# The down stage of a fused attention and feed-forward kernel: its four blocks take their accumulators in another order

## The chip, the cores and the metric

The kernel runs on one core of a Trainium2 chip. Its metric is the device time of one execution, in microseconds (us), taken as the median of several executions. A hardware profile of one execution gives the times of single instructions. In it PE is TensorE's matmul unit, PEld its weight loads, ACT is ScalarE, DVE is VectorE, POOL is GpSimd and SP is SyncE, which issues most DMAs. The span is the time from the first to the last instruction.

## The reference

Two parts follow each other. The first is a lightning attention with decay over 4 batches, 8 heads, 768 positions and a head width of 64, worked through in blocks with a running state. Its output is laid out as 3072 tokens of 512 numbers. The second is a feed-forward block:

```
out[:, :, sl] = intra + inter           # per block of positions, then kv_state is updated
x = attn_out.transpose(0, 2, 1, 3).reshape(3072, 512)
h = x @ w_in                            # 512 -> 2048
g = np.maximum(0.01 * h, h)
out = g @ w_out                         # 2048 -> 512
```

All is wanted in float32 accuracy; the weights arrive as float64.

## The kernel before

**Three products for one.** A float32 operand is split into a rounded head h, a scaled rest l and a combination m of both. A product of two operands is the matmuls h x h and l x l into one sum, scaled, and m x m into another or the same sum. So a float32 product takes three passes over PE.

**Stages.** The attention runs round by round (4 batches of 6 rounds). The up stage multiplies by `w_in`, applies the leaky ReLU and stores g to DRAM, for 6 groups of 512 tokens and 8 pairs of 128-wide slices of the hidden width (`up(g, p)`, matmul line 628). The down stage loads g back (`down_load`, line 660), splits it (ACT line 669, DVE lines 670 and 672) into a ring of four slots, and multiplies by `w_out` (`down(g, p)`, matmul line 687).

**The down stage.** A call of `down(g, p)` covers the pairs p and p + 1 of group g, for four blocks tb = 0 to 3 of 128 tokens. A block takes 12 matmuls of 512 columns for one call, six for each pair: for each half f of the pair the passes h, l and m. h and l are added into the sum `acc[tb][0]`, m into the sum `acc[tb][1]`, over the four calls of a group. In the last call of a group each block is evicted: ACT scales the first sum into `t` (line 709), DVE adds the second sum to it into `gs` (line 716), and SP stores 128 rows of the output (line 719). Both `t` and `gs` are double-buffered. After the group's fourth call the blocks start over with the next group's rows.

**The very last block** (group 5, last call, tb = 3) is ordered by hand so that its end can be worked on in halves (line 701): first all h and l matmuls of both pairs, eight in all, then the four m matmuls for columns 0 to 255, then those for columns 256 to 511. DVE adds and SP stores its rows in the same two halves.

**Accumulators.** PSUM holds these buffers: `b10`, `b11` and `b2`, one sum of 128 x 512 float32 each, which the up stage uses in rotation; `pt`, of the same size, and `psc` and `po`, each of which has room for two such sums in two halves (`psc[:, 0]` and `psc[:, 1]`). `pt`, `psc` and `po` belong to the attention before. `acc` gives each block its two sums, `ACC` the names under which the planner follows them.

**What sets the order.** Every piece of work is given to a planner (`Plan.add`) with an estimated cost, the names that it reads and writes, and a rank that grows along a list of steps. `Plan.emit` simulates the engines: at each turn it takes the piece that can start earliest, and of those that can start at the same time the one of lowest rank, then of lowest number. The pieces of one `down` call share a rank and are numbered by block. The instructions are then written out in the order of their planned starts. The waits between engines aren't the planner's: the tile framework derives them from the buffers that each instruction, in that written order, reads and writes.

The waits inside the last block come from these lines (the first part is added as usual; the halves read the name of the second sum and write that name with 0 or 1 behind it):

```
699  order = [(one, (0, 1, 2), every), (two, (0, 1, 2), every)]
700  if very_last:
701      order = [(one + two, (0, 1), every)] + [(one + two, (2,), x) for x in halves]
```

Of the kernel before, what the change touches and what calls it, by code (L numbers as in the profile page):

```python
# [36 lines left out]
class Plan:  # L37
# [23 lines left out]
    def add(self, eng, us, fn, reads=(), writes=(), rank=0.0):  # L61

        n, deps = len(self.ops), set()
        for k in reads:
            w, r = self.last.setdefault(k, [None, []])
            if w is not None:
                deps.add(w)
            r.append(n)
        for k in writes:
            w, r = self.last.setdefault(k, [None, []])  # L70
            if w is not None:
                deps.add(w)
            deps.update(r)
            self.last[k] = [n, []]
        deps.discard(n)
        ways = {eng: us} if isinstance(eng, str) else dict(zip(eng, us))
        if self.slack:
            self.more[n] = self.slack
        if self.chain is not None:
            self.chains[self.chain].append(n)  # L80
        self.ops.append((ways, fn, deps, (self.rank + rank, n), set(writes)))
# [81 lines left out]
def kernel(  # L163
# [48 lines left out]
    def ps(shape, name):  # L212
        return psum.tile(shape, F32, name=name, tag=name)


    pt = ps([P, HP, C], "pt")
    psc = ps([P, 2, 2 * HP, C2], "psc")
    po = ps([P, 2, 2 * HP, C2], "po")
    b1, b2 = [ps([P, T], f"b1{i}") for i in range(2)], ps([P, T], "b2")
# [396 lines left out]
    def up(g, p, lo=0, hi=GC):  # L616
# [35 lines left out]
            lambda: nc.sync.dma_start(out=G[g][p].rearrange("p (f t) -> p f t", f=2)[:, :, toks], in_=y), [f"gs{jg}"], [f"G{g}{p}"], slack=GSLACK)  # L652


    acc = [[b1[0], b2], [b1[1], pt.rearrange("p y t -> p (y t)")]] + [
        [z[:, i].rearrange("p y t -> p (y t)") for i in range(2)] for z in (psc, po)]
    ACC = [["b10", "b2"], ["b11", "pt"], ["psc", "psc"], ["po", "po"]]
    ring = [[X[j // 2][z].rearrange("p k t -> p (k t)")[:, j % 2 * 2 * T:(j % 2 + 1) * 2 * T] for z in range(3)] for j in range(NR)]

    def down_load(g, p):  # L660
# [14 lines left out]
    def down(g, p):  # L675

        nonlocal n_t
        for tb in range(GC):
# [3 lines left out]
            def go(pps, zs, cols, tb=tb):  # L682
                for pp in pps:
                    j = (g * NP + pp) % NR
                    for f in range(2):
                        for z in zs:
                            nc.tensor.matmul(acc[tb][z // 2][:, cols], lhsT=ring[j][z][:, f * T + tb * P:f * T + (tb + 1) * P],  # L687
                                             rhs=W[pp][z][:, f * d_model:(f + 1) * d_model][:, cols],
                                             start=pp == 0 and f == 0 and z != 1, stop=pp == NP - 1 and f == 1,
                                             skip_group_check=True)  # L690

            def needs(pps, zs):
                return [f"{x}{z}{y}" for pp in pps for z in zs for x, y in (("r", (g * NP + pp) % NR), ("w", pp))]
# [8 lines left out]
            for pps, zs, cols in order:  # L702
                part_of = f"{halves.index(cols)}" if cols in halves else ""
                add("PE", 0.227 * 2 * len(pps) * len(zs) * (0.53 if part_of else 1.0), lambda pps=pps, zs=zs, cols=cols, go=go: go(pps, zs, cols),
                    needs(pps, ["hlm"[z] for z in zs]) + ([ACC[tb][1]] if part_of else []), sorted({ACC[tb][z // 2] + part_of for z in zs}))
            if done:
                jt, n_t = n_t % 2, n_t + 1
                t, y = tt[jt], gs[jt][:, 0, :]
                add("ACT", 0.6, lambda t=t, tb=tb: nc.scalar.activation(out=t, in_=acc[tb][0], func=AF.Copy, bias=0.0, scale=(1.0 + 1.0 / S) / U),  # L709
                    [ACC[tb][0]], [f"t{jt}"], rank=-1.5)  # L710
                rows = out[(g * GC + tb) * P:(g * GC + tb + 1) * P, :]
                n = 2 if very_last else 1
                for i in range(n):
# [3 lines left out]
                            y[:, cols], acc[tb][1][:, cols], 1.0 / WS, t[:, cols], op0=ALU.mult, op1=ALU.add),  # L717
                        [f"t{jt}", ACC[tb][1]] + ([ACC[tb][1] + str(i)] if n == 2 else []), [f"gs{jt}{i}" if n == 2 else f"gs{jt}"], rank=-1.5)
                    add("DMA", 0.8 / n, lambda rows=rows, y=y, cols=cols: nc.sync.dma_start(out=rows[:, cols], in_=y[:, cols]),
# [83 lines left out]
```

## Time and profile before

| | |
|---|---|
| median of 4 runs | 613.71 us |
| the four runs | 613.15, 613.77, 613.64, 615.08 us |
| profiled execution: its own time | 613.15 us |
| its span | 611.3 us |
| PE busy | 597.3 us (98%) |
| ACT busy | 270.9 us (44%) |
| DVE busy | 313.0 us (51%) |
| matmuls of the down stage | 344.27 us to 607.45 us |
| granted TensorE clock, mean | 0.999 |

A share of busy time is an average over stages. What a change to one place is worth is read from the rows of that place: which instruction ends last there, and what it waited for. The chain that ended last follows the execution back from its last instruction, and gives for each piece the start, the length and the instruction. In a timeline row, the bracket at the end gives the idle time of the engine before the instruction, and the engine whose work ended that wait.

### The profile page before, as it was taken

To read this page: it belongs to the slowest core of one execution; us is meant where nothing else is said; L and a number is where in the kernel's file an instruction comes from. 1 tells how busy PE (TensorE), PEld (TensorE's weight loads), DVE (VectorE), ACT (ScalarE), POOL (GpSimd) and SP (SyncE) were. 2 spreads that over 40 slices of the span, in tenths; PEclk is the share of its full clock that TensorE was granted. 3 is DMA by queue.
4 is the path that set the end of the run, shared out by engine and by line. 5 is a ranking of instruction groups with operands and counts; after the bars stand their busy time and mean duration, and the time that the engine had idled before them with its cause. 6 is when DMAs were issued, how large, how long until landed. Compare 5 with 4: busy or idle time off the path is not lost.

```text
span 611.3 us, 12915 instructions
## 1 busy us (share of the span) xinstructions
PE 597.3 (98%) x5402; PEld 495.4 (81%) x5402; DVE 313.0 (51%) x412; ACT 270.9 (44%) x434; POOL 83.6 (14%) x90
## 2 busy tenths in 40 slices
PE   7799999999999999999999999999999999999997
PEld 5587888888888888888888888888888888888885
DVE  4899980164353444335356745545454545636431
ACT  4688884444465656555576622222312313114111
POOL 1563400134242013113000000000000000000000
PEclk9999999999999999999999999999999999999999
DMA  9999876445789878886775932424333333324101
GB/s 219 221 256 267 240 203 153 139 122 149 177 221 255 221 220 214 231 245 189 281 253 203 316 125 105 170 79 142 125 109 132 114 127 120 130 94 140 68 1 69
DMA packets 141162, 104.66 MB, mean 171 GB/s; under 512 B 117040, under 2 KB 117808, under 8 KB 141104
## 3 DMA queue, kind: packets, MB, share of 16 engines
q1 hardware_dynamic: 136608, 95.44, 52.8%
q10 hardware_dynamic: 4496, 8.39, 4.4%
q8 instruction: 42, 0.69, 0.5%
q14 instruction: 16, 0.13, 0.1%
HBM read 68.16 MB, written 35.65 MB: 170 GB/s over the span
## 4 chain that ended last, share of the span: by engine, by line
PE 92%; DVE 4%; DMA 2%; ACT 0%; SPq 0%; issue 0%; POOL 0%; DVEq 0%; ACTq 0%
PE b L628 42%; PE b L687 18%; PE po L687 11%; PE psc L687 11%; PE po L312 4%; PE pt L687 4%; PE psc L312 3%; DMA att<-in_v_dram 2%; DVE w L572 1%; DVE w L573 1%; PE pt L391 1%; DVE wl L584 0%; DVE wh L581 0%; DVE att L447 0%; PE po L391 0%; DVE wm L590 0%
## 5 line engine op out<-in xcount | busy, mean ns | idle before, releaser
L669 ACT ACTIVATE xh<-att 128x1024 fp32r<-128x1024 f32 x48 | 50.9, 1061 | 146.0 <-PE po L687 144.3
L670 DVE SCALAR_TENSOR_TENSOR xl<-att,xh 128x1024 fp32r<-128x1024 f32 x48 | 58.7, 1223 | 97.9 <-ACT xh L669 97.9
L628 PE MATMUL b<-xl,wl 128*128 128x512 f32 (+1 forms) x392 | 102.8, 386 | 0.6 <-DVE wl L584 0.6
L628 PE MATMUL b<-xh,wh 128*128 128x512 f32 (+1 forms) x392 | 102.7, 386 | 0.8 <-ACT xh L495 0.8
L628 PE MATMUL b<-xm,wm 128*128 128x512 f32 (+1 forms) x392 | 103.2, 391 | 0.0
L628 PEld LDWEIGHTS b<-xh,wh 128*128 128x128 f32 x392 | 72.7, 188 | 16.1 <-ACT xh L495 0.9
L628 PEld LDWEIGHTS b<-xl,wl 128*128 128x128 f32 x392 | 72.5, 188 | 15.7 <-DVE wl L584 1.0
L628 PEld LDWEIGHTS b<-xm,wm 128*128 128x128 f32 x392 | 71.2, 188 | 14.7
L649 ACT ACTIVATE gs<-b 128x512 f32<-128x512 f32 x96 | 57.3, 598 | 47.9 <-PE b L628 43.8
L646 ACT ACTIVATE b<-b 128x512 f32<-128x512 f32 x96 | 56.0, 585 | 50.3 <-PE b L628 50.2
L687 PE MATMUL b<-wh,xh 128*128 128x512 f32 x192 | 74.7, 389 | 0.0
L687 PE MATMUL b<-wl,xl 128*128 128x512 f32 x192 | 74.7, 389 | 0.0
L672 DVE SCALAR_TENSOR_TENSOR xm<-xl,xh 128x1024 fp32r<-128x1024 f32 x48 | 58.8, 1226 | 5.2 <-DVE xl L670 0.5
L440 DVE TENSOR_TENSOR att<-psc,att 128x512 f32<-128x512 f32 x24 | 16.5, 689 | 63.5 <-PE psc L312 63.3
L687 PEld LDWEIGHTS b<-wl,xl 128*128 128x128 f32 x192 | 36.1, 188 | 7.5
L687 PEld LDWEIGHTS b<-wh,xh 128*128 128x128 f32 x192 | 36.0, 188 | 7.5
L407 POOL TENSOR_TENSOR att<-att 128x512 f32<-128x512 f32 (+1 forms) x23 | 26.1, 1136 | 97.6 <-PE po L391 54.3
L572 DVE TENSOR_SCALAR w<-w 128x512 int32<-128x512 int32 x32 | 19.3, 603 | 39.3 <-ACT w L566 39.3
L450 POOL TENSOR_TENSOR att<-att 128x256 f32<-128x256 f32 x40 | 32.3, 808 | 44.1 <-DVE att L447 44.1
L687 PE MATMUL po<-wm,xm 128*128 128x512 f32 (+1 forms) x100 | 37.2, 381 | 0.7 <-ACT raw L709 0.7
L687 PE MATMUL psc<-wh,xh 128*128 128x512 f32 x96 | 37.3, 389 | 0.0
L687 PE MATMUL psc<-wl,xl 128*128 128x512 f32 x96 | 37.3, 389 | 0.0
(73 smaller groups left out, 806.6 us busy)
## 6 DMA issues: line engine op xcount, KB each, us to landing
att<-g SPq DMA_DIRECT2D x48, 512.0 KB, 3.2
g<-gs SPq DMA_DIRECT2D x47, 512.0 KB, 3.8
raw<-in_moe_w_in_dram ACTq DMA_DIRECT2D x16, 512.0 KB, 4.8
raw<-in_moe_w_out_dram SPq DMA_DIRECT2D x16, 512.0 KB, 4.5
att<-in_k_dram SPq DMA_DIRECT2D x48, 128.0 KB, 4.5
att<-in_v_dram SPq DMA_DIRECT2D x24, 256.0 KB, 4.0
out_dram<-gs SPq DMA_DIRECT2D x23, 256.0 KB, 2.0
wo<-w SPq DMA_DIRECT2D x8, 512.0 KB, 5.7
```

The costliest lines, as they stand in the source:

```text
L312: nc.tensor.matmul(dst[HALF[cols]], lhsT=lhsT[HALF[rows]], rhs=rhs[HALF[rows]], start=start, stop=True, skip_group_check=True)
L407: lambda e="POOL": ENG[e].tensor_tensor(kr[nr], kr[nr], _bc(pow_k, 3, D)[nr], op=ALU.mult), ["fk"], [f"k{i}"])
L440: add("DVE", 0.69, lambda: nc.vector.tensor_tensor(sc, psc[:, :, lower, :], decay, op=ALU.mult), ["psc", "fk"], ["sc"])
L450: add("POOL", 0.7, lambda new=new, j=j: nc.gpsimd.tensor_tensor(state[(j + 1) % 4], new, _bc(lam_c, 2, D), op=ALU.mult), [f"st{j % 4}", "f ...
L572: add("DVE", 0.42, lambda: nc.vector.tensor_scalar(d, d, 3, None, op0=ALU.logical_shift_left), [], [key])
L628: nc.tensor.matmul(dst, lhsT=w[z][:, kk * 2 * P + f * P:kk * 2 * P + (f + 1) * P], rhs=x[z][:, kk, toks], start=start and kk == 0, stop=kk ...
L646: add("ACT", ns, lambda b=b: nc.scalar.activation(out=b, in_=b, func=AF.Copy, bias=0.0, scale=S + 1.0), [], [kb], rank=-1.5)
L649: add("ACT", ns, lambda b=b, r=r: nc.scalar.activation(out=r, in_=b, func=AF.Prelu, bias=0.0, scale=1.0 / WS, alpha=0.01), [kb], [f"gs{jg} ...
L669: add("ACT", 1.05, lambda: nc.scalar.activation(out=h, in_=graw[j], func=AF.Copy, bias=0.0, scale=NEAR), reads, wr("h"))
L670: add("DVE", 1.25, lambda: nc.vector.scalar_tensor_tensor(l, graw[j], 1.0, h.bitcast(F32), op0=ALU.mult, op1=ALU.subtract), reads + [f"rh{ ...
L672: add("DVE", 1.25, lambda: nc.vector.scalar_tensor_tensor(m, l.bitcast(F32), -S, h.bitcast(F32), op0=ALU.mult, op1=ALU.add), [f"rh{j}", f" ...
L687: nc.tensor.matmul(acc[tb][z // 2][:, cols], lhsT=ring[j][z][:, f * T + tb * P:f * T + (tb + 1) * P], rhs=W[pp][z][:, f * d_model:(f + 1) ...
```

## The change

The table of accumulators is put in another order. Blocks 0 and 1 now take the halves of `psc` and of `po`, blocks 2 and 3 take `b10` with `b2` and `b11` with `pt`. With it the last block, tb = 3, has its first sum in `b11` and its second in `pt`. Nothing else differs.

```
-    acc = [[b1[0], b2], [b1[1], pt.rearrange("p y t -> p (y t)")]] + [
-        [z[:, i].rearrange("p y t -> p (y t)") for i in range(2)] for z in (psc, po)]
-    ACC = [["b10", "b2"], ["b11", "pt"], ["psc", "psc"], ["po", "po"]]
+    acc = [[z[:, i].rearrange("p y t -> p (y t)") for i in range(2)] for z in (psc, po)] + [
+        [b1[0], b2], [b1[1], pt.rearrange("p y t -> p (y t)")]]
+    ACC = [["psc", "psc"], ["po", "po"], ["b10", "b2"], ["b11", "pt"]]
```

## The prediction

> **What bounds the kernel now.** I read the page's engine table first (PE busy 98% of the span, DVE 51%, ACT 44%), then the waits of PE from 296 us to the end, the busy time by windows, the chain of waits over the last 8 us, and the timeline of the last 11 us. The waits of PE and the down stage's window (columns of the second: the stretch, then busy time and instruction count of PE, PEld, DVE, ACT and POOL, clock, DMA share, GB/s):
>
> ```profile
> PE po L687 <- ACT raw L709: 0.7, 1, 0.7
> 344.00:606.00 262.00, 262.00 (x1158) 216.91 (x1157) 128.40 (x118) 64.13 (x73) 0.00 (x0) 1.00 0.33 115
> ```
>
> From 296 us on PE waits once, for 0.7 us; from 344 to 606 us it is busy for all of the 262.00 us at full granted clock. So in the down stage the matmuls themselves set the time, at one per 0.227 us (603.13, 603.35, 603.58 in the timeline below), and a reordering of the banks can win only where PE stands still. The end of the chain of waits shows that place (start, length, what):
>
> ```profile
> 603.97 2.07 PE po L687 x11
> 606.04 0.02 issue
> 606.06 0.61 ACT raw L709
> 606.67 0.04 issue
> 606.71 0.75 PE po L687 x4
> ```
>
> The last block is cut in three by hand (line 701): eight matmuls of the h and l parts into the first sum, four half-width ones of the m part for columns 0 to 255 of the second sum, and four for columns 256 to 511. PE ends the first half, ACT evicts the first sum, and only then does PE do the second half. PE, ACT and PE stand in a row, and DVE's two half-width additions follow. The timeline of three places says why:
>
> ```profile
> 600.41 0.39 PE L687 MATMUL b<-wl,xl 128*128 128x512 f32 x1
> 600.63 0.39 PE L687 MATMUL pt<-wm,xm 128*128 128x512 f32 x1
> 600.83 0.60 ACT L709 ACTIVATE raw<-b 128x512 f32<-128x512 f32 x1 [2.12 <-PE b L687]
> ...
> 603.13 0.39 PE L687 MATMUL psc<-wl,xl 128*128 128x512 f32 x1
> 603.35 0.39 PE L687 MATMUL psc<-wm,xm 128*128 128x512 f32 x1
> 603.78 0.60 ACT L709 ACTIVATE raw<-psc 128x512 f32<-128x512 f32 x1 [2.35 <-PE psc L687]
> ...
> 605.17 0.39 PE L687 MATMUL po<-wl,xl 128*128 128x512 f32 x1
> 605.39 0.63 PE L687 MATMUL po<-wm,xm 128*128 128x256 f32 x4
> 606.06 0.60 ACT L709 ACTIVATE raw<-po 128x512 f32<-128x512 f32 x1 [1.69 <-PE po L687]
> 606.71 0.74 PE L687 MATMUL po<-wm,xm 128*128 128x256 f32 x4 [0.69 <-ACT raw L709]
> 607.54 0.76 DVE L716 SCALAR_TENSOR_TENSOR gs<-po,raw 128x256 f32<-128x256 f32 x2 [2.44 <-PE po L687]
> ```
>
> Block 1 has its sums in two buffers, b11 and pt. ACT starts at 600.83, which is 0.03 us after the last matmul into the buffer that it reads (600.41 + 0.39 = 600.80), while the m matmul into pt still runs to 601.02. Block 2 has both sums in the buffer psc. ACT starts at 603.78, 0.04 us after the m matmul into the other sum (603.35 + 0.39 = 603.74), and not after its own (603.52). So the program's waits go by buffer. In po this costs twice: ACT's read of the first sum, ready at 605.17 + 0.39 = 605.56, waits for the first m half (606.02), and the second m half, a write to po, waits for ACT's read. The DVE half of columns 0 to 255, whose own matmuls ended at 606.02, waits for the second m half too (607.46).
>
> **The change part by part.** No instruction is added, removed or resized. Blocks 0 and 1 go from b10/b2 and b11/pt to psc and po, blocks 2 and 3 the other way. Rows, weights, order of the blocks, loads and stores stay, so no step passes another on SP's or any other queue by the edit itself; only the planner's choices at the stage's start can move, costed below.
>
> *The tail.* With b11 and pt for block 3, ACT starts at 605.56 + 0.03 = 605.59 and ends at 606.19 (0.60 from its row), beside PE. The second m half has nothing to wait for: pt is not read before. It follows the first half. Within the first half four matmuls take 0.63 from start to end, their starts 0.12 apart (605.39, 605.51, 605.63), so eight take 0.63 + 4 x 0.12 = 1.11, and PE ends at 606.50 instead of 607.46. DVE's first half then starts 0.09 later as now (607.45 to 607.54), at 606.59; ACT's result of 606.19 is there. It still waits for the second m half, because both lie in pt. What leaves the chain is 0.02 + 0.61 + 0.04 of ACT and its issue, and 0.75 - 0.48 = 0.27 of refilling PE: 0.94, by the clock times 607.54 - 606.59 = 0.95. If the second half could not overlap the first and kept its 0.75, PE would end at 606.77 and the gain would be 0.68. If DVE's first half waited only for ACT and the first m half, it would start at 606.19 + 0.07 = 606.26: a gain of 1.28, and its second half, 0.34 later at 606.60, would not be held by PE either. I take 0.95, the row of the first half being the nearest.
>
> *Behind it.* The two DVE halves (607.54, 607.88), two stores issued from 608.00 and the end at 611.3 move as they are. The store of block 2 (in a row of SP's timeline issued at 605.13, landing in about 2.0 us) is over by 607.1; the first moved store is issued near 607.05. The gs buffer that the last block writes was stored for block 1, whose DVE ended at 602.15, so its 2.0 us are over by about 604.5. No new wait there: 0.
>
> *The start of the stage.* Now the planner slips six matmuls of block 2 (psc, 344.27) and six of block 1 (b11, 345.63) between the products of the last up block, then the up block's m product (346.99), and leaves block 0 until b2 is evicted (348.76). After the change psc and po, idle since the attention, serve blocks 0 and 1, so the same gap can be filled at the same time, by block 0 and then block 0 or 1; b10/b2 come later than now, and b2's wait gets longer cover. A gain is excluded, since PE has no idle time there. A loss could come only if the up block's m product were pulled ahead of ACT's scaling, which ends at 345.50, 0.13 before PE's next free place: at most one eviction, 0.6 us. I take 0.
>
> *The group changes.* Five times a block's buffer is written again, 8.16 us (three blocks of 2.72) after its last matmul. The tightest is block 3, whose eviction stands behind conversions of the next group:
>
> ```profile
> 389.41 0.58 ACT L709 ACTIVATE raw<-po 128x512 f32<-128x512 f32 x1
> ...
> 393.12 0.68 DVE L716 SCALAR_TENSOR_TENSOR gs<-po,raw 128x512 f32<-128x512 f32 x1
> ...
> 396.86 0.39 PE L687 MATMUL po<-wh,xh 128*128 128x512 f32 x1
> ```
>
> It ends at 393.80 and PE comes back at 396.86: 3.06 us of cover, 8.16 us of distance for every block in either order. Taken as 0; if the cover went, each microsecond beyond would count five times.
>
> *A rule against the change.* The row: each sum of psc or po is 512 floats wide, in a half of its own, and ACT nevertheless waited 606.06 - 605.59 = 0.47 us for a write to the other half. The Trainium skill, PSUM — Partial Sum Buffer, section "PSUM bank collisions raise a hardware error", asks for semaphores by bank and quadrant, and the page's terms put 512 floats in a bank. By that rule the two sums were in separate banks already, nothing had to wait, and the change would be worth 0; by the rows it is worth 0.95. The same rule asks that DVE's read and PE's write within one bank be kept apart, which would leave the first DVE half waiting for the second m half, as I have it.
>
> *The sum.* The profiled execution took 613.15 with a span of 611.3, so 1.85 lies outside the span. After: span 611.3 - 0.95 = 610.35, execution 612.20. That execution is the fastest of the four, 0.56 under the median of 613.71. On the median: 613.71 - 0.95 = 612.76, or 612.8, which is 0.15%.
>
> **The rivals.**
> 1. *DVE's first half is released early* and the tail gives 1.28: 612.4. For it: its own matmuls end 0.48 earlier. Against: at 607.54 it waited for the second half although its columns were done at 606.02, and pt is one buffer for both.
> 2. *The separation doesn't do what it says:* 613.7. It would need ACT's wait to be something other than the shared buffer. Against are blocks 1 and 2 above, which differ in just that.
> 3. *Slower:* at the five group changes the eviction of block 3 falls behind another pair of conversions on DVE (four at 1.23 us, 4.92), so that b11 and pt come free 4.92 - 3.06 = 1.86 late, five times: 9.3 - 0.95 = 8.4 slower, 622.1. It decides from a delay of 0.44 beyond the cover (5 x 0.44 = 2.2, less 0.95, is 1.25). For it: the planner lays out both queues anew. Against: the block distances and lengths are unchanged, and the next conversion starts only at 397.97 on ACT, when a ring slot comes free.
> 4. *A smaller gain* of 0.3 to 0.7, by the unoverlapped second half or 0.6 lost at the start: 613.0 to 613.4.
>
> **How the numbers follow.** A measurement of this kernel can tell about 0.2%, 1.23 us, from no change. The forecast (a gain of 0.95) has 0.74, rival 1 0.09, rival 2 0.05, rival 3 0.06, rival 4 0.06. The forecast lies only 0.28 inside the bound, and the four runs differ by 0.1 to 0.6 us even without the 615.08; so I give about four in ten of its 0.74 to a time beyond the bound (0.30), the rest to within it (0.44). Of rival 1, 0.07 is beyond and 0.02 within; rivals 2 and 4 are within, less 0.02 for runs as high as 615.08. Faster 0.37, same 0.02 + 0.44 + 0.11 - 0.02 = 0.55, slower 0.08. The range goes from 612.1 (rival 1 less 0.3 of spread) to 613.4 (rival 4's upper end); rivals 2 and 3 and the far ends of the spread are left out.
>
> **What would show it.** Right: in the last block ACT starts about 0.03 after the last l matmul and beside the m halves, PE has no wait after 296 us, eight half-width matmuls follow each other in about 1.1 us, DVE starts 0.09 after the last, and the span is near 610.35. The waits list would lose PE <- ACT. Wrong: an ACT start after the first m half again (rival 2), a DVE start before the last m matmul ends (rival 1), or PE waits for DVE L716 near 396 us and every 43.5 us after (four pairs of 10.88) (rival 3). A change anywhere ahead of 344 us would overturn the reading that the plan is the same up to there.

## The result and the profile after

The changed kernel takes 613.05 us (median of 33 runs, 611.78 to 615.11); the kernel before, in 53 runs, takes 613.9 us. The ratio is 0.9987 with a 95% interval of 0.9982 to 0.9992, which is 0.5 to 1.1 us faster. That is 0.13%, inside the 0.2% that the prediction called no change. The profiled execution took 612.5 us, its span is 610.7 us.

The end of the chain of waits of the changed kernel (start, length, what; DVEq is DVE's sequencer):

```profile
605.89 0.96 PE pt L688 x8
606.86 0.03 DVEq L717
606.89 0.04 issue
606.93 0.42 DVE gs L717
```

ACT is gone from the chain, and the eight m matmuls of the last block are one piece. (All lines of the code are one further down than before.) The timeline of the last block:

```profile
605.50 0.39 PE L688 MATMUL b<-wl,xl 128*128 128x512 f32 x1
...
605.73 1.11 PE L688 MATMUL pt<-wm,xm 128*128 128x256 f32 x8
605.93 0.60 ACT L710 ACTIVATE raw<-b 128x512 f32<-128x512 f32 x1 [1.44 <-PE b L688]
606.93 0.75 DVE L717 SCALAR_TENSOR_TENSOR gs<-pt,raw 128x256 f32<-128x256 f32 x2 [1.73 <-PE pt L688]
```

ACT starts 0.04 us after the last l matmul (605.50 + 0.39 = 605.89) and runs beside the m matmuls. The waits of PE from 296 us on no longer have one on ACT. The one row that is left belongs to the attention:

```profile
PE po L312 <- DVE att L479: 0.3, 1, 0.3
```

It isn't new: the same wait of 0.28 us ends at 295.54 us in the kernel before and, because this execution runs 0.34 us later, at 295.88 us here.

The execution can be cut at three marks that every trace has: the start of the first down matmul, the start of the last l matmul, and the start of DVE's first half. The **stage** lies between the first two, the **tail** between the second and the third, and the **rest** from there to the end of the span. (The page prints the span to 0.1 us; the spans here are the kept traces' own, to 0.01.)

| profiled execution | first down matmul | stage | tail | rest | span |
|---|---|---|---|---|---|
| before | 344.27 | 260.90 | 2.37 | 3.79 | 611.33 |
| changed | 344.61 | 260.89 | 1.43 | 3.79 | 610.72 |

The tail gives 0.94 us. This execution came to the down stage 0.34 us later, through code that the change does not touch, so its span shows only 0.6 of it.

### The profile page after: what moved, and what is told of

It reads as the page before. It is cut to its first block, busy times and chain, and to the rows that moved or that the text cites. A ratio compares the mean times of both kernels' runs of the same rounds, so it can differ in the third digit from the quotient of the medians.

```text
span 610.7 us, 12915 instructions
## 1 busy us (share of the span) xinstructions
PE 597.8 (98%) x5402; PEld 495.5 (81%) x5402; DVE 313.2 (51%) x412; ACT 270.7 (44%) x434; POOL 83.2 (14%) x90
## 4 chain that ended last, share of the span: by engine, by line
PE 92%; DVE 3%; DMA 3%; SPq 0%; issue 0%; POOL 0%; ACT 0%; DVEq 0%; ACTq 0%
PE b L628 42%; PE b L688 18%; PE po L688 11%; PE psc L688 11%; PE po L312 4%; PE pt L688 4%; PE psc L312 3%; DMA att<-in_v_dram 2%; DMA att<-in_k_dram 1%; DVE w L573 1%; DVE wm L590 1%; DVE wl L584 0%; DVE w L572 0%; DVE wh L581 0%; PE po L391 0%; PE pt L391 0%
## 5 line engine op out<-in xcount | busy, mean ns | idle before, releaser
L572 DVE TENSOR_SCALAR w<-w 128x512 int32<-128x512 int32 x32 | 17.1, 533 | 40.2 <-ACT w L566 40.1
L688 PE MATMUL psc<-wm,xm 128*128 128x512 f32 x96 | 37.3, 389 | 0.0
```

What stands on the lines that cost most here:

```text
L572: add("DVE", 0.42, lambda: nc.vector.tensor_scalar(d, d, 3, None, op0=ALU.logical_shift_left), [], [key])
```

## The experiments

Two theories stood against each other from the start. The first: waits go by buffer, and the whole gain is the tail of the last block. The second: the gain comes from elsewhere, from the banks in which the stage begins or from where the sums lie in PSUM. Ratios below are to runs of the kernel before on the same chip; each run's kernel was timed 12 times, the two with the cut in every group 7 and 10 times.

**Another pair of buffers at the end.** (In this run and the next, both tables are built from a list of names; shown is what comes out for one of them.)

```
-    ACC = [["b10", "b2"], ["b11", "pt"], ["psc", "psc"], ["po", "po"]]
+    ACC = [["po", "po"], ["b11", "pt"], ["psc", "psc"], ["b10", "b2"]]      # acc alike
```

> Blocks 0 to 3 take po, b11/pt, psc, b10/b2: the last block has its two sums in two buffers again, but other ones, and the stage begins with other banks than in either kernel. Theory (waits go by buffer, the whole gain is in the tail): from the start of the last l matmul to the start of DVE's first half 1.43 us as in the changed kernel (2.37 before), so 0.94 us faster than before, ratio near 0.9985. Rival (the gain comes from which bank the stage starts in, or from b11 and pt as such): the tail or the stage's length differs from the changed kernel's and the gain is lost or halved, 0 to 0.5 us.

Ratio 0.9979 (0.9967 to 0.9991). The stage took 260.89 and the tail 1.43 us. It is not b11 and pt that matter, and not the banks at the start.

**A new order with the last block in one buffer.**

```
-    ACC = [["b10", "b2"], ["b11", "pt"], ["psc", "psc"], ["po", "po"]]
+    ACC = [["po", "po"], ["b10", "b2"], ["b11", "pt"], ["psc", "psc"]]      # acc alike
```

> Blocks 0 to 3 take po, b10/b2, b11/pt, psc: the order of the buffers is new everywhere, and the last block's two sums share the buffer psc. Theory: the tail of before comes back, 2.37 us from the last l matmul to DVE's first half with PE waiting 0.7 us for ACT, and the time equals that of before within 0.1 us (ratio 1.000). Rival (the gain comes from the stage's new start, or po alone was at fault): 0.5 to 0.95 us faster than before.

Ratio 0.9999 (0.9985 to 1.0012). The end of its chain of waits is that of before, in psc instead of po:

```profile
606.63 0.61 ACT raw L713
607.23 0.04 issue
607.28 0.75 PE psc L691 x4
608.03 0.04 DVEq L720
```

The stage took 260.89, the tail 2.38 us. So all blocks can change their banks and nothing moves as long as the last one keeps its two sums in one buffer. These two runs together show the cause.

**The m matmuls in one go, in the kernel before.**

```
-                order = [(one + two, (0, 1), every)] + [(one + two, (2,), x) for x in halves]
+                order = [(one + two, (0, 1), every), (one + two, (2,), every)]
```

> The kernel before, but the last block's m matmuls are done in one go at full width (four instead of eight; DVE and the stores keep their halves). Theory: PE waits for nothing; ACT's read of the first half of po waits for all four m matmuls, whose last ends 0.22 + 3 x 0.227 + 0.39 = 1.29 us after the last l matmul's start, then ACT 0.60 and DVE: 0.04 + 0.60 + 0.06 later. So 1.99 us from the last l matmul to DVE instead of 2.37: 0.38 us faster than before (ratio 0.9994). If ACT did not wait by buffer, it would run beside the m matmuls and DVE would start after 1.29 + 0.09 = 1.38 us: 0.99 us faster.

Ratio 0.9986 (0.9974 to 0.9997). The interval holds both the 0.9994 of the theory and the 0.9984 of its rival, so the trace decides:

```profile
603.79 2.73 PE po L687 x12
606.52 0.02 issue
606.55 0.60 ACT raw L709
607.15 0.03 issue
607.18 0.42 DVE gs L716
```

ACT waits for all of the m matmuls, as a wait by buffer has it, and the tail is 1.96 us (1.99 expected). So 0.41 of the 0.94 us (2.37 - 1.96) were the price of cutting the m matmuls inside a shared buffer. The other 0.53 (1.96 - 1.43) are ACT standing behind PE instead of beside it, 0.58, less the 0.05 that the cut still costs in the changed kernel (next run).

**The same in the changed kernel.**

> The changed kernel with the last block's m matmuls in one go at full width. Theory (DVE's first half waits for all that is written to pt, so the cut of the m matmuls serves nothing): DVE starts 1.29 + 0.09 = 1.38 us after the last l matmul's start instead of 1.43, 0.05 us faster than the changed kernel, 0.99 faster than before (ratio 0.9984). Rival (the cut lets DVE's first half go early): the first half starts later than 1.43, by up to 0.3 us, and the time is above the changed kernel's by as much.

The edit is the one above. Ratio 0.9983 (0.9972 to 0.9995), tail 1.38 us. The cut of the m matmuls serves nothing in the changed kernel either; without it the tail is 0.05 us shorter. This settles the prediction's first rival: DVE's first half never went early.

**The two sums crossed between blocks 2 and 3.**

```
+    acc_last = acc[:2] + [[acc[2][0], acc[3][1]], [acc[3][0], acc[2][1]]]   # used in group 5
+    ACC_last = ACC[:2] + [["psc", "po"], ["po", "psc"]]
```

> The kernel before, but in the last group blocks 2 and 3 swap their second sums: block 2 has psc[0] and po[1], block 3 has po[0] and psc[1]. Each sum stays in a half of 512 floats of its own, as before; only the buffer that the last block's second sum belongs to is another than its first sum's. Theory (waits go by buffer): ACT's last eviction runs beside the m halves, PE has no wait, DVE's first half starts 1.43 us after the last l matmul instead of 2.37: 0.94 us faster than before (ratio 0.9985). The eviction of block 2 by DVE (its second sum now lies in po) waits until block 3's l matmuls end and starts about 1.2 us later than before, which is not on the path. Rival (the place of the two sums in PSUM counts, not the buffer's name; before, they were in two separate halves already): nothing changes, 0 us.

Ratio 1.0019 (1.0010 to 1.0028): about 1.2 us slower by the ratio, 0.8 by the marks of the trace, which neither theory said. The timeline of PE shows why:

```profile
605.08 0.63 PE L690 MATMUL psc<-wm,xm 128*128 128x256 f32 x4
606.39 0.74 PE L690 MATMUL psc<-wm,xm 128*128 128x256 f32 x4 [0.69 <-ACT raw L712]
607.12 0.51 PE L690 MATMUL po<-wh,xh 128*128 128x512 f32 x1
```

With these names the planner took the h and l matmuls to be held by block 2's eviction and put the two m halves ahead of them. The second half then waited 0.69 us for ACT's read of block 2's sum in the other half of psc, and the eviction of block 3 came last, behind the h and l matmuls. The run tests another written order and not the question, except that the wait of 0.69 us in the shared buffer is there again, for another pair of instructions.

**Crossed, with the order of before.** The buffers are crossed as above, but the planner is told the old names (and, for the group's first call, that block 2 also writes `po`).

> As the crossed kernel (in the last group block 2 has psc[0] and po[1], block 3 has po[0] and psc[1]), but the planner keeps the names of before for them, so that the written order of the last call is that of before: h and l of block 3, then the two m halves. Theory (waits go by buffer): ACT's last eviction starts 0.03 us after the last l matmul's end and runs beside the m halves, PE has no wait, DVE's first half starts 1.43 us after the last l matmul's start instead of 2.37, and the time is 0.94 us below before (ratio 0.9985). DVE's eviction of block 2 reads the half of po next to the one that block 3's h and l matmuls write, so it waits for their end, about 1.2 us later than before. Rival (the place of the sums in PSUM counts): the two sums were in separate halves before and still are, so nothing changes: 2.37 us, 0 us.

Ratio 0.9989 (0.9978 to 1.0000), stage 260.89, tail 1.84 us: a gain of 0.53, neither 0.94 nor 0. PE has no wait and the eight m matmuls follow each other, as the theory has it; the rival is out. The chain shows what was left out of the expectation:

```profile
604.99 2.05 PE po L688 x9
607.05 0.04 DVEq L717
607.08 0.04 issue
607.13 0.70 DVE gs L717
607.83 0.02 issue
607.85 0.61 ACT raw L710
608.46 0.02 issue
608.48 0.42 DVE gs L717
```

DVE's eviction of block 2, whose second sum now lies in po, waited for block 3's h and l matmuls in the other half, as expected. But ACT's eviction of block 3 waited for that DVE instruction too, 0.03 us behind its end, though both only read po. They have one more buffer in common: ACT writes one half of `raw`, which holds both `t`, while DVE reads the other. But in SBUF, the memory that holds `t` and the ring, two halves of one buffer aren't kept apart here. In the same trace ACT writes one ring slot of `xh` while PE reads the slot that is the other half of that buffer:

```profile
388.56 1.06 ACT L669 ACTIVATE xh<-att 128x1024 fp32r<-128x1024 f32 x1 [0.31 <-PE po L688]
388.82 0.39 PE L688 MATMUL po<-wh,xh 128*128 128x512 f32 x1
```

So it is `po` that ACT waits for: the program keeps even two reads apart when they come from two engines and lie in one PSUM buffer. The runs have this in one place only. The Trainium skill, PSUM — Partial Sum Buffer, section "PSUM bank collisions raise a hardware error", lists reads against reads among what must not meet, but within one bank and quadrant; the runs show the waits across the two halves of a buffer, 512 floats each.

**The cut in every group.**

```
-            very_last = done and g == NG - 1 and tb == GC - 1
+            very_last = done and tb == GC - 1        # and the names of the gs halves, so that the order holds
```

> The kernel before, with the last block's order (h and l of both pairs first, then m in two halves, DVE and stores in halves) in block 3 of every group, not of the last alone. It multiplies the disputed wait by about six. Theory (waits go by buffer): at five group changes the second m half waits for ACT's read of po, which stands behind a conversion of 1.06 us that itself waits for block 3's l matmuls; so it starts about 1.06 + 0.60 + 0.1 = 1.75 us after the l matmuls' end instead of 0.48, some 1.3 us lost each time: 5 x 1.3 + 5 x 0.05 for the narrower matmuls = 6.7 us slower than before (range 3 to 12), PE waiting for ACT about six times. Rival (no wait by buffer): 0.3 us slower, no waits.

> The changed kernel with the same order in block 3 of every group. Theory: the first sum is in b11, the second in pt, so PE has no wait at any group change; 0.05 us a group for the narrower matmuls: 0.3 us slower than the changed kernel, about 0.65 us faster than before, and some 7 us faster than the same edit on the kernel before. Rival (the wait is not by buffer): as slow as the same edit on the kernel before.

On the kernel before the ratio is 1.0018 (1.0000 to 1.0037), on the changed kernel 0.9986 (0.9973 to 0.9999). The stage took 261.26 us in both, 0.36 more than without, which is 0.07 for each of the five cuts (0.05 expected). The tails are 2.37 and 1.43. So this expectation failed: the 6.7 us are not there. In the trace of the first, PE waits for ACT only in the last block, in that of the second not at all, and the two differ behind the start of the stage by the 0.94 us of their tails, as the two kernels without this edit do. A group change in the kernel before, with this edit:

```profile
389.30 1.12 PE L687 MATMUL po<-wm,xm 128*128 128x256 f32 x8
...
390.45 0.60 ACT L709 ACTIVATE raw<-po 128x512 f32<-128x512 f32 x1
```

The eight m matmuls run through. At a group change ACT's eviction stands behind two conversions in the plan, so its read is written out after both halves and PE need not wait for it. By the rows ACT starts 0.03 us behind the second half (389.30 + 1.12 = 390.42). In the last block nothing stands before ACT, its read is planned between the halves, and the second half has to wait. The shared buffer alone does not cost PE time; a read written between two writes does.

**Two queues for the last stores.** The changed kernel, m matmuls in one go, and the second output half stored from ACT's queue:

```
+   q = nc.scalar if i else nc.sync      # i: output half; q.dma_start(out=rows[:, cols], in_=y[:, cols])
```

> The changed kernel with the last block's m matmuls in one go, and its second output half stored from ACT's queue instead of SP's. Theory: the tail up to DVE is 1.38 us. SP's second issue stands 0.13 us behind the end of DVE's second half because the first issue takes 0.33 us and more (608.29 to 608.42 before); ACT's queue is free, so the second issue comes about 0.09 us sooner: the part from DVE's start to the end goes from 3.8 to 3.7 us, in all 1.05 to 1.1 us below before (ratio 0.9983). Rival (an issue from ACT costs more, or the two stores then collide): that part stays at 3.8 us or grows, 0.8 to 0.99 below before.

Ratio 0.9975 (0.9962 to 0.9988), median 612.87 us beside 614.45 of before. The second issue now stands directly behind DVE's second half (609.49 + 0.41 = 609.90):

```profile
609.49 0.41 DVE L717 SCALAR_TENSOR_TENSOR gs<-pt,raw 128x256 f32<-128x256 f32 x1
609.61 0.33 SPq L720 DMA_DIRECT2D out_dram<-gs  x1
609.94 0.37 ACTq L720 DMA_DIRECT2D out_dram<-gs  x1
```

Tail 1.39 and rest 3.70 make 5.09 us, beside 5.22 of the changed kernel and 6.16 of before. That is 1.07 us less than before, where 1.05 to 1.1 was expected, and 0.13 less than the changed kernel. The measured times can't tell the last: the intervals overlap.

## Why the prediction was right, and where its terms were off

- *What bounds the kernel.* PE ran through the stage in 260.90 us before and 260.89 after. A reordering could win only in the one wait of PE, and did.
- *The tail.* Predicted: ACT 0.03 us after the last l matmul, eight m matmuls in 1.11 us, DVE 0.09 behind them, a gain of 0.95. In the trace: 0.04, 1.11 us, and DVE at 606.93 after 605.73 + 1.11 = 606.84, which is 0.09; the gain is 0.94. The first m half was the right row to take.
- *Behind it.* The rest was to move as it is: 3.79 and 3.79.
- *The start of the stage.* Taken as 0, with block 0 filling the gap. In the chain after, both pairs of block 0 run there and then the up block's m matmuls, with no wait:

```profile
344.77 2.72 PE psc L688 x12
347.49 0.91 PE b L628 x4
348.40 2.72 PE po L688 x12
```

- *The group changes.* Block 3's eviction ends at 394.13 and PE comes back to the block at 397.20, 3.07 us later, where 3.06 was predicted. The cover is even longer, which the prediction overlooked: that DVE instruction reads `pt`, which PE writes again only at 397.65, 3.52 us later. And `b11`, which PE writes at 397.20, has been free since ACT's read ended at 390.33. The slower rival had its place right there and did not come.
- *The rule by banks.* It would have made the change worth 0. The waits of this program in PSUM go by buffer and not by bank, so it did not bear on them.
- *The rivals.* The early release of DVE's first half is refuted by its start behind the last m matmul, in the changed kernel and without the cut. (Its 0.07 us from ACT's end to DVE is 0.03 in the run without the cut, 607.15 to 607.18, so its gain would have been 1.32 and not 1.28.) That the separation does nothing is refuted by the two runs with other orders. The smaller gain is refuted only by the trace: the measured 613.05 us lies in that rival's own 613.0 to 613.4, but the second m half does overlap the first (1.11 us for eight) and the stage loses nothing at its start. On the measured time alone, the forecast and this rival could not be told apart.
- *The numbers.* 612.8 was predicted and 613.05 measured. Most of the 0.25 us is the base: 53 runs put the kernel before at 613.9 and not 613.71. By the ratio the gain is 0.80 us (0.13% of 613.9), and its interval, 0.49 to 1.10, holds 0.95.

## What to carry to other kernels

When two sums are evicted at different moments, give them two PSUM buffers, not two halves of one, wherever an engine must write the one while another reads the other; look for it at the very end, where no other work covers the wait. Such a wait costs only where the read is written out between two writes, so look at the order of the instructions, not at the buffer alone. And a last step that is cut into halves to start the next engine earlier pays only if the next engine is really released by the half: here the cut cost 0.41 us in the shared buffer and 0.05 us in separate ones.

## What the runs showed beside this

In the profiles, what varies from one execution to the next lies almost wholly ahead of the down stage. In the eight profiled executions with the down stage's matmuls in the original shape and order (before, changed, and the runs with other buffer orders, without the cut, crossed with the order of before, and with two queues), the first down matmul started between 344.27 and 346.87 us, while the stage took 260.89 or 260.90 in each. A change in this stage of a few tenths of a microsecond can be read from marks in one trace, where the measured time needs dozens of runs.

One thing stays open: the rest is 3.47 us in the two kernels with the cut in every group, 3.71 without the cut in the kernel before and in the first crossed kernel, 3.70 with two queues, and 3.78 or 3.79 in all others. With two queues the second issue comes 0.79 us after DVE's start (609.94 - 609.15) instead of 0.88 (608.42 - 607.54), which is as much as the rest is shorter; for the others no run shows why.
